# One decode step of gated attention plus MLP: fewer matmul instructions, two weight blocks moved in the load order

## The chip, the cores and the metric

The kernel runs on one core of a Trainium2 chip. The metric is device microseconds (us) of one execution. In what follows TensorE is called PE, VectorE DVE, ScalarE ACT, and SyncE SP; SP issues nearly all DMAs.

## The reference, cut to what matters

Two batch rows, one token each, D = 448, 16 heads of size 256, 4096 cached positions; all in float32.

```python
g = sigmoid((x * gate_w).sum(-1, keepdims=True))
q = (x @ wq).reshape(B, 1, 16, 256)
scores = einsum("bhqd,bhkd->bhqk", q, k_cache) * 256 ** -0.5
a = einsum("bhqk,bhkd->bhqd", softmax(scores), v_cache) @ wo
h = relu(x @ w1 + b1)
b = (h * h) @ w2 + b2
out = g * a + (1 - g) * b
```

The caches are 134 MB each, so nearly all of the 289.5 MB that the kernel reads is K and V, each byte of which is used once.

## The kernel before, in words

**Rounds.** The work is cut into 16 rounds, numbered 0 to 15 (`rounds`, `last` = 15). Round i is one batch row and one pair of heads; the two heads lie on the upper and the lower 64 partitions, 64 positions to a partition. Each round needs a K tile in two halves (`k{i}_0`, `k{i}_1`, 4 MB each, loaded by `load_k`, L141) and a V tile of 8 MB (`load_v`, L146; in round 15 `load_v_last` loads it as `va` and three pieces of `vb`, L152 and L156).

**What a round does.** DVE multiplies K by q in place (`times_q`, L303) and sums rows (`row_sums`, L308): two passes over each half. `maximum` (L312, L316) takes each partition's maximum and lets PE spread it over the partitions of its head; `softmax` reduces that to a negated maximum `nb` on DVE (L322) and exponentiates on ACT (L327). `values` (L353) multiplies the probabilities by V on PE with 32 matmuls, of which the trace shows two records each. `make_q` (L260, L263) spreads the q of the round after next over the partitions with PE and copies it with ACT. A few multiplications of the next round's K stand between the steps of the softmax, so that DVE needn't wait for PE.

**Units and output.** After a unit of four heads (after rounds 3, 7, 11) and after the last two pairs (rounds 13 and 15), `take` and `turn` (L367, L381, L390) bring the outputs on partitions; `project` (L394) multiplies four heads by their part of `wo`, accumulating in `acc` over 448 columns. For the last four heads (12 to 15) `late_wo`, and for the late blocks of `w2` `late_w2`, do the same product by `late` (L399), as four matmuls of 112 columns each into four row groups of `fin`. `w2` has 14 blocks of 224 KB; the first `WH` of them are multiplied into `acc` in round 4 (L472), the others at the very end. `ya` (L478) is the copy of `acc` that a `late` of its own adds to `fin`. Then `y4` (L500) leaves by two small DMAs.

**Memory and order of loads.** The order is written out by hand. SP issues the loads in program order, and each waits until its buffer is free. All of K, `w1`, `w2`, `wo` and `va` go through a ring of three buffers of 32 KB a partition; V, `wq` and `vb` share one buffer of 64 KB a partition. So V of round i is issued when PE is done with V of round i-1, and a half of K when DVE is done with the tile three ring places earlier. In round i SP issues V of round i, then extra weights if any, then `k{i+1}_1` and `k{i+2}_0`. The last K is issued in round 13; rounds 14 and 15 load V, the last part of `wo` (L125) and the late `w2` (L108).

Of the kernel before, what the change touches and what calls it, by code (L numbers as in the profile page):

```python
# [8 lines left out]
F32 = mybir.dt.float32  # L9
AF = mybir.ActivationFunctionType  # L10
ALU = mybir.AluOpType
# [5 lines left out]
def kernel(  # L17
# [32 lines left out]
    NQ = N // QB  # L50
    assert QB == 2 * DH
    DQ = D // 4
    WH = 2
    W2_CUTS = (4, 8, 11)
    V_CUTS = (48, 56)
    LEAD = 4
    LEAD2 = 16
# [11 lines left out]
    def slot(name):  # L69
        return ring.tile([P, J * DH], F32, name=name, tag="ring")  # L70
# [19 lines left out]
    w2_v = w2.rearrange("(p c) n -> p c n", c=FC)  # L90
    w2_sb = {}

    def w2_slot(lo, hi):
        t = slot(f"w2_{lo}")
        tv = t[:, :(hi - lo) * D].rearrange("p (c n) -> p c n", n=D)
        for c in range(lo, hi):
            w2_sb[c] = tv[:, c - lo, :]
        return tv

    def load_w2_early():  # L100
        tv = w2_slot(0, WH)
        nc.sync.dma_start(tv, w2_v[:, :WH, :])

    def load_w2_late():
        tv = w2_slot(WH, FC)
        at = [0, *W2_CUTS, FC - WH]
        for lo, hi in zip(at, at[1:]):
            nc.sync.dma_start(tv[:, lo:hi, :], w2_v[:, WH + lo:WH + hi, :])  # L108

# [4 lines left out]
    wo_sb = {}  # L116

    def load_wo(g):
        t = slot(f"wo{g}")
        tv = t[:, :HJ * D]  # L120
        if g < NG - 1:
            nc.sync.dma_start(tv, wo_g[g])
            wo_sb[g] = tv.rearrange("p (j n) -> p j n", j=HJ)
        else:
            nc.sync.dma_start(tv.rearrange("p (h k) -> p h k", h=HG), wo_v[:, g * HG:(g + 1) * HG, :])  # L125
            wo_sb[g] = tv.rearrange("p (h j n) -> p h j n", h=HG, j=NJ)


    rounds = [(b, n) for n in range(H // 2) for b in range(B)]
# [123 lines left out]
    def make_q(i):  # L253

        b, n = rounds[i]
        a, g = divmod(n, NQ // 2)
        r = 32 * g + B * a + b
        pq = ps.tile([P, 512], F32, name=f"pq{i}", tag="pq")
        for k in range(2):
            nc.tensor.matmul(pq[k * PH:(k + 1) * PH, :DH], ident[:, r:r + 1].to_broadcast([P, PH]),  # L260
                             qs[:, k * DH:(k + 1) * DH], start=True, stop=True)
        q_sb[i] = work.tile([P, DH], F32, name=f"q{i}", tag=f"q{b}")
        nc.scalar.activation(q_sb[i], pq[:, :DH], AF.Copy)  # L263


    hT = const.tile([P, FC, B], F32, name="hT")
# [43 lines left out]
    def maximum(i):  # L310
        m = work.tile([P, 1], F32, name=f"m{i}", tag="m")
        nc.vector.tensor_reduce(m, s_t[i], axis=AX.X, op=ALU.max)  # L312
        mt = ps.tile([P, 512], F32, name=f"mt{i}", tag="sm")
        for k in range(2):
            at = slice(k * PH, (k + 1) * PH)
            nc.tensor.matmul(mt[at, :PH], m.to_broadcast([P, PH]), ident[:, at], start=True, stop=True)  # L316
        return mt

    def softmax(i, mt):
        b, n = rounds[i]  # L320
        nb = work.tile([P, 1], F32, name=f"nb{i}", tag="nb")
        nc.vector.tensor_reduce(nb, mt[:, :PH], axis=AX.X, op=ALU.max, negate=True)  # L322
        u, k = unit_of[2 * n]
        for e in range(2):
            at = slice(e * PH, (e + 1) * PH)
            c = B * (k + e) + b
            nc.scalar.activation(pw[k, b][at, :, 2 * c:2 * c + 2], s_t[i][at].rearrange("p (m s) -> p m s", s=2), AF.Exp,  # L327
                                 bias=nb[at], accum_out=rs_t[u % 2][at, c:c + 1])
# [62 lines left out]

    def project(g):
        for j in range(HJ):
            nc.tensor.matmul(acc[:, :D], oT[g][:, j, :], wo_sb[g][:, j, :], start=False,  # L394
                             stop=(g == NG - 2 and j == HJ - 1))

    def late(lt, rhs, start=False, stop=False):
        for k in range(4):
            nc.tensor.matmul(fin[32 * k:32 * k + B, :DQ], lt, rhs[:, k * DQ:(k + 1) * DQ], start=start, stop=stop)  # L399

    def late_wo(h):
        u, k = unit_of[h]
        for j in range(NJ):
            late(oT[u][:, j, B * k:B * k + B], wo_sb[NG - 1][:, h % HG, j, :])

    def late_w2(lo, hi):
        for c in range(WH + lo, WH + hi):
            late(hT[:, c, :], w2_sb[c], stop=(c == FC - 1))
# [17 lines left out]
    for i, (b, n) in enumerate(rounds):  # L426
# [5 lines left out]
        if i == 1:  # L432
            w1_t = load_w1()
        if i == 4:
            load_w2_early()
        if done and u < NG - 1:
            load_wo(u)
        if i == last - 1:
            load_wo(NG - 1)
        if i == last:  # L440
            load_w2_late()
        if i < last - 1:
            load_k(i + 1, 1)
            load_k(i + 2, 0)
# [9 lines left out]
        if done:  # L454
            norm(u, sums(u))
        if i == last:
            break
        values(i, vt)

# [12 lines left out]
                nc.tensor.matmul(acc[:, :D], hT[:, c, :], w2_sb[c], start=False, stop=False)  # L472
        if i + 2 <= last:
            make_q(i + 2)
        if i == last - 3:

            ya = const.tile([B, D], F32, name="ya")
            nc.scalar.activation(ya, acc[:, :D], AF.Copy)  # L478
            late(ident[:B, :B], ya, start=True)
        if i == last - 1:  # L480
            late_wo(H - 4)
            late_wo(H - 3)
        rest(i + 1)
        if i == 2:
            ffn_square(pt)
# [6 lines left out]
    values(last, vt[1], p3, NK // 2)  # L492
    take(NG)
    turn(NG)
    late_w2(0, W2_CUTS[0])
    late_wo(H - 2)
    late_wo(H - 1)
    late_w2(W2_CUTS[0], FC - WH)
    y4 = const.tile([P, DQ], F32, name="y4")
    nc.scalar.activation(y4, fin[:, :DQ], AF.Copy)  # L500
    ov = out.rearrange("b s (k n) -> b k (s n)", k=4)
# [29 lines left out]
```

## Time and profile before

| | |
|---|---|
| median of 3 runs | 682.19 us (682.14 to 683.8) |
| the profiled execution, its own time | 683.37 us |
| its span, first to last instruction | 681.5 us |
| busy: DVE, PE, ACT | 571.7, 242.7, 35.4 us |
| read from memory | 289.56 MB |
| busy share of 16 DMA engines by the SP queue | 98.9% |

The span is measured between the first and the last instruction; 1.9 us of the profiled time lie around it. The clock column in the rows below is the clock granted to TensorE, as a share of 2.4 GHz: 0.50 is its 1.2 GHz level.

### The profile page before, as it was taken

The page shows a single profiled execution, that of the slowest core. Times are in us where ns is not written, and L with a number is a line of the kernel's source. Part 1 is how long each engine was busy: PE and PEld are TensorE (multiplying, and loading weights), DVE is VectorE, ACT ScalarE, POOL GpSimd, SP SyncE. Part 2 cuts the span into 40 slices and gives each one's busy share as a digit, 9 for nine tenths or more (in the row PEclk, how much of TensorE's full clock was granted, in tenths as well). Part 3 has the DMA queues.
Part 4 walks back from the last instruction along what each step waited for, and adds up shares of the span by engine and source line. Part 5 has one row for each costly group of instructions (what it writes and reads, how often), then busy time and mean ns, then how long its engine had stood idle before and what let it go on. Part 6 is the DMA issues. An engine that isn't in the chain of part 4 may idle for free.

```text
span 681.5 us, 3765 instructions
## 1 busy us (share of the span) xinstructions
PE 242.7 (36%) x1618; PEld 83.6 (12%) x1618; DVE 571.7 (84%) x171; ACT 35.4 (5%) x110; POOL 0.7 (0%) x6
## 2 busy tenths in 40 slices
PE   2500506308158150504028450321406523060066
PEld 1100101004014010101004110000103100010023
DVE  3199999597987979798895979989795997989970
ACT  0100000100001000000001000000001000000000
POOL 0000000000000000000000000000000000000000
PEclk9955856758566585756657775565858757585589
DMA  9999999999999999999999999999999999999996
GB/s 378 435 458 419 430 456 410 453 410 427 456 397 454 415 447 439 411 456 412 450 407 433 442 420 442 425 444 423 443 435 413 450 414 452 413 431 451 400 409 251
DMA packets 9500, 289.79 MB, mean 425 GB/s; under 512 B 1158, under 2 KB 1292, under 8 KB 2316
## 3 DMA queue, kind: packets, MB, share of 16 engines
q1 hardware_dynamic: 9320, 289.54, 98.9%
q8 instruction: 12, 0.20, 0.1%
q10 hardware_dynamic: 164, 0.02, 0.0%
q14 instruction: 4, 0.03, 0.0%
HBM read 289.56 MB, written 0.00 MB: 425 GB/s over the span
## 4 chain that ended last, share of the span: by engine, by line
DMA 62%; DVE 21%; PE 16%; issue 0%; ACT 0%; SPq 0%
DMA v<-in_A_v_cache_dram 51%; PE po_buf L353 15%; DVE k L303 10%; DVE s L308 10%; DMA k<-in_A_k_cache_dram 6%; DMA wq<-in_A_wq_dram 3%; DMA w<-in_B_w_dram 2%; PE po_buf L223 1%; PE fin L399 0%; PE pq L260 0%; ACT qs L249 0%; SPq L108 0%; DVE nb L322 0%; ACT q L263 0%; SPq L141 0%
## 5 line engine op out<-in xcount | busy, mean ns | idle before, releaser
L303 DVE TENSOR_TENSOR k<-k,q 128x4096 f32<-128x4096 f32 (+3 forms) x63 | 281.6, 4485 | 81.5 <-DMA k<-in_A_k_cache_dram 62.1
L308 DVE TENSOR_REDUCE s<-k 128x32 f32<-128x8192 f32 x32 | 277.9, 8686 | 1.1
L353 PE MATMUL po_buf<-v,pw 128*16 128x512 f32 (+1 forms) x960 | 137.7, 738 | 150.6 <-DMA v<-in_A_v_cache_dram 150.6
L316 PE MATMUL mt<-ident,m 128*64 128x64 f32 x64 | 7.6, 329 | 248.3 <-DVE m L312 248.3
L353 PEld LDWEIGHTS po_buf<-v,pw 128*16 128x16 f32 (+1 forms) x960 | 30.9, 111 | 246.0 <-issue 209.6
L316 PEld LDWEIGHTS mt<-ident,m 128*64 128x64 f32 x64 | 5.0, 201 | 255.2 <-issue 212.4
L327 ACT ACTIVATE pw<-s,nb 64x64 f32<-64x64 f32 x32 | 11.2, 349 | 287.7 <-DVE nb L322 287.4
L394 PE MATMUL acc<-wo,oT 128*2 128x448 f32 x48 | 24.3, 673 | 2.5 <-ACT oT L387 2.5
L381 PE MATMUL ot<-rl,shared 128*128 128x8 f32 x96 | 17.7, 322 | 5.2 <-ACT shared L363 5.2
L381 PEld LDWEIGHTS ot<-rl,shared 128*128 128x128 f32 x96 | 17.2, 278 | 8.3 <-ACT shared L363 8.3
L263 ACT ACTIVATE q<-pq 128x256 f32<-128x256 f32 x16 | 6.1, 383 | 198.7 <-PE pq L260 198.6
L260 PE MATMUL pq<-qs,ident 128*64 128x256 f32 x64 | 10.7, 418 | 0.7 <-ACT qs L249 0.7
L223 PE MATMUL po_buf<-wq,xT 128*4 128x512 f32 x56 | 8.7, 791 | 4.9 <-DMA wq<-in_A_wq_dram 4.9
L363 ACT ACTIVATE shared<-po_buf 128x1024 f32<-128x1024 f32 x6 | 5.8, 1021 | 55.2 <-PE po_buf L353 55.2
L284 PEld LDWEIGHTS pt<-ident,shared 4*128 4x128 f32 x28 | 6.9, 336 | 0.9 <-issue 0.9
L284 PE MATMUL pt<-ident,shared 4*128 4x4 f32 x28 | 7.0, 380 | 0.0
L394 PEld LDWEIGHTS acc<-wo,oT 128*2 128x2 f32 x48 | 4.5, 98 | 20.1 <-issue 17.4
L353 PE MATMUL po_buf<-va,pw 128*8 128x512 f32 x32 | 6.2, 947 | 0.0
L327 ACT ACTIVATION_READ_ACCUMULATOR pw<-s,nb 64x1 f32 x32 | 5.9, 185 | 0.0
L333 PE MATMUL sum<-rs,ones_pp 128*128 128x8 f32 (+1 forms) x10 | 3.0, 369 | 8.1 <-ACT pw L327 8.1
L223 PE MATMUL ph<-w,xT 128*4 128x448 f32 x28 | 5.4, 539 | 0.0
L260 PEld LDWEIGHTS pq<-qs,ident 128*64 128x64 f32 x64 | 3.3, 138 | 11.6 <-issue 9.7
(64 smaller groups left out, 60.5 us busy)
## 6 DMA issues: line engine op xcount, KB each, us to landing
k<-in_A_k_cache_dram SPq DMA_DIRECT2D x32, 4096.0 KB, 31.0
wq<-in_A_wq_dram SPq DMA_DIRECT2D x1, 7168.0 KB, 19.8
wo<-in_A_wo_dram SPq DMA_DIRECT2D x4, 1792.0 KB, 33.7
va<-in_A_v_cache_dram SPq DMA_DIRECT2D x1, 4096.0 KB
w<-in_B_w_dram SPq DMA_DIRECT2D x1, 3136.0 KB, 32.3
vb<-in_A_v_cache_dram SPq DMA_DIRECT2D x1, 2048.0 KB
vb<-in_A_v_cache_dram SPq DMA_DIRECT2D x2, 1024.0 KB, 13.1
w<-in_B_w_dram SPq DMA_DIRECT2D x2, 896.0 KB, 13.6
```

Source lines behind the costliest of these rows:

```text
L223: nc.tensor.matmul(out[32 * g:32 * g + 2 * B, :width], xT[:, half, c].rearrange("p s b -> p (s b)"), t[:, (a * n + g) * width:(a * n + g + ...
L260: nc.tensor.matmul(pq[k * PH:(k + 1) * PH, :DH], ident[:, r:r + 1].to_broadcast([P, PH]), qs[:, k * DH:(k + 1) * DH], start=True, stop=True)
L263: nc.scalar.activation(q_sb[i], pq[:, :DH], AF.Copy)
L284: nc.tensor.matmul(pt[:, c, :], hv[:, c, :], ident[:2 * B, :2 * B], start=True, stop=True)
L303: nc.vector.tensor_tensor(kt, kt, q_sb[i].unsqueeze(1).to_broadcast([P, hi - lo, DH]), op=ALU.mult)
L308: nc.vector.tensor_reduce(s_t[i][:, half * J:(half + 1) * J], kts[i, half], axis=AX.X, op=ALU.add)
L316: nc.tensor.matmul(mt[at, :PH], m.to_broadcast([P, PH]), ident[:, at], start=True, stop=True)
L327: nc.scalar.activation(pw[k, b][at, :, 2 * c:2 * c + 2], s_t[i][at].rearrange("p (m s) -> p m s", s=2), AF.Exp, bias=nb[at], accum_out=rs_ ...
L353: nc.tensor.matmul(po[r:r + 4 * n, :], pw[k, b][:, m, :4 * n], vt[:, 2 * m:2 * m + 2, :].rearrange("p j d -> p (j d)"), start=(k == 0 and ...
L363: nc.scalar.activation(o_w[:, s], po_bufs[u % 2][:, s * DH:(s + 1) * DH].rearrange("r (p j) -> r j p", j=HJ).unsqueeze(2).to_broadcast([P, ...
L381: nc.tensor.matmul(ptv[:, j, :], ov[:, s, j, :], rl_t[u][:, :, s], start=(s == 0), stop=(s == 1))
L394: nc.tensor.matmul(acc[:, :D], oT[g][:, j, :], wo_sb[g][:, j, :], start=False, stop=(g == NG - 2 and j == HJ - 1))
```

## The change

- `make_q`: one matmul of 128x512 instead of two of 64x256; then ACT copies each half of the partitions by itself (two copies instead of one).
- `maximum` and `softmax`: one matmul of 128x128 instead of two of 64x64; then DVE reduces each half of the partitions by itself (two reductions instead of one).
- `w2`: eight blocks instead of two are loaded and multiplied in round 4, six instead of twelve at the end, in pieces of three, two and one.
- `wo` of heads 12 and 13 is loaded alone in round 14 and multiplied into `acc` behind `values` of round 14 (`project_pair`); `ya` is copied after that, and the `late` that adds it to `fin` stands in round 15 between the sums and the last `values`.
- `wo` of heads 14 and 15 is loaded behind the last V, into the ring buffer that the late `w2` has too (`end`), and multiplied ahead of the late `w2`.

```diff
-    WH = 2
-    W2_CUTS = (4, 8, 11)
+    WH = 8
+    W2_CUTS = (3, 5)
...
+    def load_wo_pair(t, h):
+        tv = t[:, :2 * NJ * D].rearrange("p (h k) -> p h k", h=2)
+        nc.sync.dma_start(tv, wo_v[:, h:h + 2, :])
+        for k in range(2):
+            wo_h[h + k] = tv[:, k, :].rearrange("p (j n) -> p j n", j=NJ)
...
+        nc.tensor.matmul(pq, ident[:, r:r + 1].to_broadcast([P, P]), qs, start=True, stop=True)
+        q_sb[i] = work.tile([P, DH], F32, name=f"q{i}", tag=f"q{b}")
         for k in range(2):
-            nc.tensor.matmul(pq[k * PH:(k + 1) * PH, :DH], ident[:, r:r + 1].to_broadcast([P, PH]),
-                             qs[:, k * DH:(k + 1) * DH], start=True, stop=True)
-        q_sb[i] = work.tile([P, DH], F32, name=f"q{i}", tag=f"q{b}")
-        nc.scalar.activation(q_sb[i], pq[:, :DH], AF.Copy)
+            at = slice(k * PH, (k + 1) * PH)
+            nc.scalar.activation(q_sb[i][at], pq[at, k * DH:(k + 1) * DH], AF.Copy)
...
-        for k in range(2):
-            at = slice(k * PH, (k + 1) * PH)
-            nc.tensor.matmul(mt[at, :PH], m.to_broadcast([P, PH]), ident[:, at], start=True, stop=True)
+        nc.tensor.matmul(mt[:, :P], m.to_broadcast([P, P]), ident, start=True, stop=True)
...
-        nc.vector.tensor_reduce(nb, mt[:, :PH], axis=AX.X, op=ALU.max, negate=True)
+        for e in range(2):
+            at = slice(e * PH, (e + 1) * PH)
+            nc.vector.tensor_reduce(nb[at], mt[at, at], axis=AX.X, op=ALU.max, negate=True)
...
+    def project_pair(h):
+        u, k = unit_of[h]
+        for e in range(2):
+            for j in range(NJ):
+                nc.tensor.matmul(acc[:, :D], oT[u][:, j, B * (k + e):B * (k + e + 1)], wo_h[h + e][:, j, :], start=False,
+                                 stop=(e == 1 and j == NJ - 1))
...
         if i == 4:
-            load_w2_early()
+            load_w2(slot("w2a"), 0, WH)
...
         if i == last - 1:
-            load_wo(NG - 1)
+            load_wo_pair(slot("wo12"), H - 4)
         if i == last:
-            load_w2_late()
+            t = slot("end")
+            load_wo_pair(t, H - 2)
+            load_w2(t[:, 2 * NJ * D:], WH, FC, W2_CUTS)
...
         if i == last:
+            late(ident[:B, :B], ya, start=True)
             break
...
-        if i == last - 3:
-
+        if i == last - 1:
+
+            project_pair(H - 4)
             ya = const.tile([B, D], F32, name="ya")
             nc.scalar.activation(ya, acc[:, :D], AF.Copy)
-            late(ident[:B, :B], ya, start=True)
-        if i == last - 1:
-            late_wo(H - 4)
-            late_wo(H - 3)
...
-    late_w2(0, W2_CUTS[0])
     late_wo(H - 2)
     late_wo(H - 1)
-    late_w2(W2_CUTS[0], FC - WH)
+    late_w2(0, FC - WH)
```

**SP's queue in rounds 3 to 5.** First before, then changed; `v_514` is V of round 4, the `k` names behind it are the second half of round 5 and the first of round 6.

```order
L146 DMA v_514<-in_A_v_cache_dram 128x16384
L102 DMA w_0_516<-in_B_w_dram 128x896
L141 DMA k_1_518<-in_A_k_cache_dram 128x8192
L141 DMA k_0_520<-in_A_k_cache_dram 128x8192
L146 DMA v_577<-in_A_v_cache_dram 128x16384
```

```order
L140 DMA v_514<-in_A_v_cache_dram 128x16384
L99 DMA w2a<-in_B_w_dram 128x3584
L135 DMA k_1_518<-in_A_k_cache_dram 128x8192
L135 DMA k_0_520<-in_A_k_cache_dram 128x8192
L140 DMA v_583<-in_A_v_cache_dram 128x16384
```

The load of `w2` ahead of all later K has 3584 columns of float32 a partition instead of 896.

**SP's queue at the end.** First before, then changed; `k_1_1143` is the last K, `v_1214` is V of round 14.

```order
L141 DMA k_1_1143<-in_A_k_cache_dram 128x8192
L146 DMA v_1214<-in_A_v_cache_dram 128x16384
L125 DMA wo_1216<-in_A_wo_dram 128x4x896
L152 DMA va<-in_A_v_cache_dram 128x8192
L156 DMA vb<-in_A_v_cache_dram 128x4096
L156 DMA vb<-in_A_v_cache_dram 128x2048 x2
L108 DMA w_2_1288<-in_B_w_dram 128x1792 x2
L108 DMA w_2_1288<-in_B_w_dram 128x1344
L108 DMA w_2_1288<-in_B_w_dram 128x448
```

```order
L135 DMA k_1_1143<-in_A_k_cache_dram 128x8192
L140 DMA v_1214<-in_A_v_cache_dram 128x16384
L118 DMA wo_1216<-in_A_wo_dram 128x2x896
L146 DMA va<-in_A_v_cache_dram 128x8192
L150 DMA vb<-in_A_v_cache_dram 128x4096
L150 DMA vb<-in_A_v_cache_dram 128x2048 x2
L118 DMA end<-in_A_wo_dram 128x2x896
L99 DMA end<-in_B_w_dram 128x1344
L99 DMA end<-in_B_w_dram 128x896
L99 DMA end<-in_B_w_dram 128x448
```

Half of the last `wo` load stands behind `vb` now, and of `w2` there are three pieces of 2688 columns together instead of four of 5376.

**PE's queue from the maximum of round 14 on.** First before, then changed; `v_1214` is V of round 14, `mt_1295` and `mt_1285` are round 15's maxima.

```order
L316 MATMUL mt_1220<-ident,m_1218 64x64 x2
L353 MATMUL po_buf_92<-v_1214,pw_0_99 8x512 x32
L399 MATMUL fin<-wo_1216,oT_1202 2x112 x16
L316 MATMUL mt_1295<-ident,m_1293 64x64 x2
L333 MATMUL sum_1302<-rs_107,ones_pp 128x4
L353 MATMUL po_buf_92<-va,pw_1_101 8x512 x16
L353 MATMUL po_buf_92<-vb,pw_1_101 8x512 x16
L381 MATMUL ot_1343<-rl_1307,o_1341 128x4 x4
L399 MATMUL fin<-w_2_1288,hT 2x112 x16
L399 MATMUL fin<-wo_1216,oT_1348 2x112 x16
L399 MATMUL fin<-w_2_1288,hT 2x112 x32
```

```order
L308 MATMUL mt_1220<-ident,m_1218 128x128
L347 MATMUL po_buf_92<-v_1214,pw_0_99 8x512 x32
L394 MATMUL acc<-wo_1216,oT_1202 2x448 x4
L308 MATMUL mt_1285<-ident,m_1283 128x128
L327 MATMUL sum_1292<-rs_107,ones_pp 128x4
L399 MATMUL fin<-ya,ident 2x112 x4
L347 MATMUL po_buf_92<-va,pw_1_101 8x512 x16
L347 MATMUL po_buf_92<-vb,pw_1_101 8x512 x16
L375 MATMUL ot_1337<-rl_1297,o_1335 128x4 x4
L399 MATMUL fin<-end,oT_1342 2x112 x16
L399 MATMUL fin<-end,hT 2x112 x24
```

Behind the last `ot` stand 40 matmuls instead of 64, all of them `wo` first; the four on `ya` stand ahead of the last `values`.

## Rows read from the trace of the kernel before

**Rows 1.** The page: the span, and two DMA queues (packets, MB, share of 16 engines).
```profile
span 681.5 us, 3765 instructions
...
q1 hardware_dynamic: 9320, 289.54, 98.9%
q8 instruction: 12, 0.20, 0.1%
```

**Rows 2.** A stretch: length, busy of PE, PEld, DVE, ACT, POOL, clock, DMA share, GB/s.
```profile
300.00:500.00 200.00, 66.61 (x410) 21.53 (x410) 177.51 (x44) 8.93 (x31) 0.00 (x0) 0.63 1.00 433
```

**Rows 3.** Who waited for whom: us in total, times, longest.
```profile
DVE k L303 <- DMA k<-in_A_k_cache_dram: 62.1, 13, 8.0
```

**Rows 4.** The chain that ended last: start us, us, what (pieces of it).
```profile
119.34 35.79 DMA v<-in_A_v_cache_dram
...
193.97 9.96 PE po_buf L353 x64
...
246.02 30.90 DMA v<-in_A_v_cache_dram
...
514.47 8.44 PE po_buf L353 x64
...
567.47 39.53 DMA k<-in_A_k_cache_dram
...
625.82 0.13 DVE nb L322
...
660.47 16.64 DMA w<-in_B_w_dram
```

**Rows 5.** The instructions from 600 us on: start us, us, which [idle before <-releaser].
```profile
607.02 8.69 DVE L303 TENSOR_TENSOR k<-k,q 128x8192 f32<-128x8192 f32 x1 [3.32 <-DMA k<-in_A_k_cache_dram]
...
655.20 1.28 SPq L156 DMA_DIRECT2D vb<-in_A_v_cache_dram  x3
...
659.63 0.22 DVE L312 TENSOR_REDUCE m<-s 128x1 f32<-128x64 f32 x1
...
662.16 6.18 PE L353 MATMUL po_buf<-va,pw 128*8 128x512 f32 x32
...
668.17 3.61 PE L353 MATMUL po_buf<-vb,pw 128*8 128x512 f32 x32
...
673.54 0.95 PE L399 MATMUL fin<-w,hT 128*2 128x112 f32 x32
673.64 0.18 ACT L390 ACTIVATE oT<-ot 128x8 f32<-128x8 f32 x1 [1.20 <-PE ot L381]
...
675.07 0.95 PE L399 MATMUL fin<-w,hT 128*2 128x112 f32 x32
...
677.15 0.95 PE L399 MATMUL fin<-w,hT 128*2 128x112 f32 x32 [1.13 <-DMA w<-in_B_w_dram]
```

**Rows 6.** Groups by shape: xcount, busy us, mean ns, idle before.
```profile
L260 PE MATMUL pq<-qs,ident 128*64 128x256 f32 x64 | 10.7, 418 | 0.7 <-ACT qs L249 0.7
L263 ACT ACTIVATE q<-pq 128x256 f32<-128x256 f32 x16 | 6.1, 383 | 198.7 <-PE pq L260 198.6
L472 PE MATMUL acc<-w,hT 128*2 128x448 f32 x4 | 1.7, 539 | 0.0
L399 PE MATMUL fin<-ya,ident 2*2 2x112 f32 x8 | 0.4, 253 | 1.0 <-ACT ya L478 1.0
```

**Rows 7.** DMA issues: xcount, KB each, median us to landing.
```profile
w<-in_B_w_dram SPq DMA_DIRECT2D x1, 448.0 KB, 17.1
```

**Rows 8.** Stretches near the end, columns as in rows 2.
```profile
658.00:660.00 2.00, 0.00 (x1) 0.04 (x1) 1.81 (x2) 0.00 (x0) 0.00 (x0) 1.00 1.05 410
...
662.00:664.00 2.00, 2.00 (x14) 0.58 (x17) 0.51 (x3) 0.00 (x0) 0.00 (x0) 0.50 0.96 397
...
668.00:670.00 2.00, 2.00 (x24) 0.50 (x20) 0.00 (x0) 0.00 (x0) 0.00 (x0) 1.00 1.00 422
...
676.00:678.00 2.00, 0.87 (x35) 0.60 (x32) 0.00 (x0) 0.00 (x0) 0.00 (x0) 1.00 0.05 18
```

More of the change, by code (lines that the diff above doesn't have):

```diff
@@ L91, with load_w2 @@
     w2_sb = {}
-    def w2_slot(lo, hi):
-        t = slot(f"w2_{lo}")
+    def load_w2(t, lo, hi, cuts=()):
         tv = t[:, :(hi - lo) * D].rearrange("p (c n) -> p c n", n=D)
@@ L97, in w2_slot @@
             w2_sb[c] = tv[:, c - lo, :]
[L98 to L108, printed above, removed]
+        at = [0, *cuts, hi - lo]
+        for a, e in zip(at, at[1:]):
+            nc.sync.dma_start(tv[:, a:e, :], w2_v[:, lo + a:lo + e, :])
     HJ = HG * DH // P
@@ L118, in load_wo @@
     def load_wo(g):
[L119 to L126, printed above, removed]
+        tv = slot(f"wo{g}")[:, :HJ * D]
+        nc.sync.dma_start(tv, wo_g[g])
+        wo_sb[g] = tv.rearrange("p (j n) -> p j n", j=HJ)
+    wo_h = {}
+    def load_wo_pair(t, h):
[3 more added lines that the diff above has]
+            wo_h[h + k] = tv[:, k, :].rearrange("p (j n) -> p j n", j=NJ)
     rounds = [(b, n) for n in range(H // 2) for b in range(B)]
@@ L393, in project @@
         for j in range(HJ):
-            nc.tensor.matmul(acc[:, :D], oT[g][:, j, :], wo_sb[g][:, j, :], start=False,
-                             stop=(g == NG - 2 and j == HJ - 1))
+            nc.tensor.matmul(acc[:, :D], oT[g][:, j, :], wo_sb[g][:, j, :], start=False, stop=False)
+    def project_pair(h):
[4 more added lines that the diff above has]
+                                 stop=(e == 1 and j == NJ - 1))
     def late(lt, rhs, start=False, stop=False):
@@ L403, in late_wo @@
         for j in range(NJ):
-            late(oT[u][:, j, B * k:B * k + B], wo_sb[NG - 1][:, h % HG, j, :])
+            late(oT[u][:, j, B * k:B * k + B], wo_h[h][:, j, :])
     def late_w2(lo, hi):
```

## The prediction

> **What bounds the kernel now.** I read the page's DMA queues first. SP's queue keeps 16 engines busy for 98.9% of the span [rows 1], and a long stretch in the middle shows a share of 1.00 at 433 GB/s [rows 2]. So the loads run one behind the other, without a hole, and when a tile lands is set by how many bytes stand ahead of it. Next I read who waits. DVE waited 13 times for a K tile, 62.1 us in all [rows 3]: it is faster than the loads and falls in step with them in every round. The last such wait is the one to remember: the second half of round 14's K landed at 607.0 us, after DVE had been idle for 3.32 us [rows 5]. The chain shows the same load, issued at 567.47 and 39.53 us under way [rows 4].
>
> From 607.02 on there are two paths to the end, and the timeline of the tail shows both [rows 5]. **The loads' path:** behind that K tile the queue still brings two halves of K, all of V of round 14, the last `wo`, V of round 15 and twelve blocks of `w2`; the third piece of `w2` is what PE waited for until 677.15, with 1.13 us of idle time. **The computing path:** DVE works without a gap from 607.02 until the last maximum, which starts at 659.63; the softmax of round 15 lets PE start the last `values` at 662.16; they end at 668.17 + 3.61 = 671.78; `oT` is ready at 673.64 + 0.18 = 673.82; then the final products follow. The loads' path ends last, but the computing path is only 1.13 us short of it. That slack is what this change has to be held against.
>
> **The change part by part.**
>
> *Six blocks of `w2` move from the end of the queue to round 4.* Two blocks are 448 KB [rows 7], so six are 1344 KB, 1.376 MB; at 433 GB/s [rows 2] that is 3.18 us. They are removed behind the last V and added ahead of every K and V from round 5 on. The sum of bytes is the same, so the end of the loads' path stays where it is. But every later K lands 3.18 us later, the one at 607.02 with them, at about 610.2. DVE was waiting for it and works without a gap afterwards, so nothing takes this up: **+3.18 us on the computing path**. From below: DVE's idle time before that tile is 3.32 us only because the earlier K are just as late; if part of the shift were taken up, it would be at rounds in which DVE doesn't wait, and there are none late in the run, so I take the whole. From above: 1.376 MB at 397 GB/s, the slowest of the busy stretches shown [rows 8], is 3.47 us. The Trainium skill (DMA: Bandwidth & Descriptors, section Where 436 GB/s comes from) says that loads from HBM are held to about 358 GB/s for a core; the rows show 433, so the trace disagrees. By the page's figure the blocks would cost an estimated 3.84 us, and the sum below would be 0.7 us more.
>
> PE's six further products in round 4 are 12 records at 1.7 us for 4 records [rows 6], under 5.1 us, behind `values` of round 4. SP's load of the ring buffer that they free waits for them; behind it stand the next loads. The cover is the queue: V issued at 246.02 landed 30.90 us later [rows 4], of which its own 8.39 MB take 19.4 us at 433 GB/s, so 11.5 us of older loads were still queued. Price 0 to 0; without that cover it would be up to 5.1 us.
>
> *Order of the last loads.* Half of the last `wo` (two heads, 0.92 MB, 2.1 us) goes behind V of round 15. The issue of `vb` waits for `values` of round 14, as before (655.20, [rows 5]), and its wait moves with everything else by 3.2 us. With less `wo` ahead of it, engines that run early may run dry for up to 2.1 us before `vb` comes. That is off the path, if the computing path ends last; the floor of the loads' path is the last landing. The `wo` of heads 14 and 15 lies ahead of `w2`, whose third piece was 16.64 us under way [rows 4]; it is needed only at the final products: 0.
>
> *One matmul and two copies for q.* The same columns go through PE (64 records of 256 become 32 of 512), and ACT gets one more copy of about 0.38 us in each round [rows 6]. From round 2 on, q is ready two rounds ahead: 0. The first q delays DVE's first product by about 0.4 us. SP's issues wait for DVE in the first rounds, but V issued at 119.34 landed 35.79 us later [rows 4], 16.4 us more than its own bytes take: the queue is deep, so 0; with an empty queue it would be 0.4.
>
> *One matmul and two reductions for the maximum.* PE's part has the same columns. DVE gets a second reduction per round, whose step in the chain is 0.13 us [rows 4]. In rounds 0 to 13 the waits for K, or in the first rounds the deep queue, hide it. In rounds 14 and 15 nothing does: **+0.26 us** (0.13 if ACT's first exponential starts after the first reduction).
>
> *`ya` moves in front of the last `values`.* Eight records, 0.4 us busy in all [rows 6] at the high clock, stand between the sums and `values`. They are pipelined with what follows, so **+0.3 us** (0.2 to 0.5). The products of heads 12 and 13 follow `values` of round 14 in both kernels, while PE waits for DVE: 0.
>
> *The last `values`.* Before they took 671.78 - 662.16 = 9.62 us: the granted clock had fallen from 1.00 to 0.50 (the 1.2 GHz level) after PE had little to do, and the `va` half took 6.18 us, the `vb` half at 1.00 3.61 us [rows 5, 8]. In the eleven earlier rounds that the chain lists with 64 records they took 8.44 to 9.96 us [rows 4], 9.13 in the mean. PE again has some 4 us with almost nothing to do before them, so the clock should fall again; when it rises within them is open. I take 9.13: **-0.49 us** (-1.18 to +0.34).
>
> *The final products.* Before, 6.32 us passed from the end of `values` (671.78) to the end of the last product (677.15 + 0.95 = 678.10). In the changed kernel `oT` takes the same 2.04 us. Then come 40 matmuls, 80 records. Records went through at 32 in (675.07 - 673.54) / 2 = 0.765 us [rows 5], so 1.91 us, and about 0.2 to drain: 4.15 us. **-2.17 us.** No `w2` fills the pause before `oT` any more; that is in the 4.15.
>
> *The sum.* Computing path: 3.18 + 0.26 + 0.3 - 0.49 - 2.17 = **+1.08 us** against the end at 678.10. Loads' path: the last landing stays at about 677.1 to 677.7, and only the last block (8 records, 0.2 us) can stand behind it, so it ends at about 677.95, 0.15 us before the old end. The computing path is now the later one, by 1.2 us. The profiled execution (span 681.5, its own time 683.37) would become 684.45. Its time lies 1.18 us above the median of the runs, 682.19; the difference carries over, so I forecast **683.3 us**, 0.16% above 682.19.
>
> **The rivals.** About 0.3%, 2.05 us, is what a measurement of this kernel can tell from no change.
>
> *A. The loads stay the bound.* If PE stays at the high clock through the last `values`, they take 2 x 3.61 = 7.2 us instead of 9.13, and the computing path ends 1.9 us sooner, at 677.3, ahead of the last `w2`. Then the loads' path decides: 682.19 - 0.15 = 682.0. For it: the clock was still 1.00 from 658 to 660 with an idle PE [rows 8], and the products of heads 12 and 13 take PE a little further. Against it: the clock did fall in the same pause before the last `values` [rows 8], and over the long stretch its mean is 0.63 [rows 2], as it would be if every pause brought it down.
>
> *B. Slower by more than 0.3%: PE late and slow in the last round.* The place is `values` of round 15 and the products behind it. If the clock rises late, `values` take 9.96 us as in the slowest round [rows 4]: +0.83 us, or 684.1. From 0.97 us above the forecast on it counts as slower, so another 0.14 us decides. That comes if the 80 final records find the clock at 0.50 for even a tenth of their way; all of them at 0.50 would be +1.9, or 686.0. For it: the path has no slack left in front of the output, so each tenth counts. Against it: at the end before, the clock stayed at 1.00 even through the wait of 1.13 us.
>
> *C. Fewer instructions help the queue.* PE fetches its instructions over the same DMA engines: 12 packets, 0.20 MB, 0.1% of the 16 engines' span [rows 1], or 0.00 to 0.15% at most, some 10.9 us of one engine, 0.9 us each. The change takes out 16 + 16 matmuls in the rounds, 12 by `wo` and 18 by `w2`, 62 in all; each is two matmul and two weight-load records, so 248 instructions. If each packet delays the engine that finishes last, the tiles come sooner by up to 0.9 us, and the time is 682.4; together with A it is 681.1. The Trainium skill (Runtime: NRT & Kernel Launch, section Instruction fetch mechanics) says that a sequencer refills in blocks of 256 instructions by its own DMA queue and that this is mostly hidden; the 12 packets of the trace agree with the block size, and by the page the gain would be an estimated one packet. Against a gain beyond 0.3%: it needs more than two packets on one engine.
>
> **How the numbers follow.** The forecast (computing path ends last, within 0.3%) has 0.62. A has 0.14, at 682.0, and also counts as same. B has 0.18, at 684.3 to 686. C in a form that brings more than 0.3%, below 680.1, has 0.03, and what I haven't seen 0.03, of which I give 0.01 to faster, 0.01 to same and 0.01 to slower. So same is 0.62 + 0.14 + 0.01 = 0.77, slower 0.19, faster 0.04. The range runs from the loads' floor, 682.0 less 0.2 for C, 681.8, up to 684.9 in B: the sum with the upper ends of its terms (3.47 for the shift, 0.5 for `ya`, +0.34 for `values`) is 3.47 + 0.26 + 0.5 + 0.34 - 2.17 = 2.40, 684.6, and 0.3 for a little of the final products at the low clock. About 0.1 lies above it and 0.06 below.
>
> **What would show it.** In the profile of the changed kernel: the wait of DVE for round 14's second half of K ends about 3 us later (610 instead of 607); the last maximum is at about 663; the last `values` start near 666; PE no longer waits for `w2` in the final products, and the chain of waits leads from the output through `fin`, `values` and DVE back to K instead of to the load of `w2`; the DMA share falls to nothing before the final products start. q8 shows 11 or 12 packets. It would be wrong if DVE's work after the last K started less than 2 us later, if the last `values` took 7.2 us, or if the chain still ended in a `w2` load.

## The result: slower, by 0.46%

| | median | runs |
|---|---|---|
| before | 682.18 us | 681.88 to 683.8 (10) |
| changed | 685.66 us | 683.82 to 687.06 (10) |
| ratio | 1.0046 | 95% interval 1.0031 to 1.0062 |

The forecast was 683.3 us, no measurable change, in a range up to 684.9; the time is 2.4 us above the forecast and outside the range. The ten runs of the changed kernel lie in two groups, five from 683.82 to 684.7 and five from 686.63 to 687.06, with nothing between them. So the median, 685.66 us, lies in the gap and is no execution's time; the medians of the two groups are 684.36 and 686.92 us, and the ratio of the two overall medians would be 1.0051. The profiled execution, 687.06 us with a span of 685.3, is from the upper group. Two more profiles of the kernel stand below, after_b and after_c; after_c, 684.17 us, is from the lower group.

The instructions of the changed kernel's profile (687.06 us) that answer to [rows 5]; columns are start, duration, instruction, idle time before it:

```profile
610.51 8.69 DVE L297 TENSOR_TENSOR k<-k,q 128x8192 f32<-128x8192 f32 x1 [2.42 <-DMA k<-in_A_k_cache_dram]
...
629.22 0.47 DVE L316 TENSOR_REDUCE nb<-mt 64x1 f32<-64x64 f32 x2
629.72 7.69 DVE L297 TENSOR_TENSOR k<-k,q 128x3072 f32<-128x3072 f32 x2
...
663.49 0.22 DVE L306 TENSOR_REDUCE m<-s 128x1 f32<-128x64 f32 x1
...
666.14 0.55 PE L399 MATMUL fin<-ya,ident 2*2 2x112 f32 x8
...
666.62 6.00 PE L347 MATMUL po_buf<-va,pw 128*8 128x512 f32 x32
...
672.44 3.61 PE L347 MATMUL po_buf<-vb,pw 128*8 128x512 f32 x32
...
678.14 1.60 PE L399 MATMUL fin<-end,oT 128*2 128x112 f32 x32 [0.27 <-ACT oT L384]
...
679.50 2.40 PE L399 MATMUL fin<-end,hT 128*2 128x112 f32 x48
```

DVE's last wait for K ends 3.49 us later than in [rows 5], and everything that follows is late with it. At the end no product waits for `w2` any more: only `oT` is waited for. The loads were done before: the rows below show a DMA share of 0.07 in the stretch before the products, and of 0.00 and 0.03 while they run. They also show the clock (columns as in [rows 2]):

```profile
658.00:660.00 2.00, 2.00 (x16) 0.42 (x5) 2.00 (x1) 0.00 (x0) 0.00 (x0) 1.00 0.25 98
...
676.00:678.00 2.00, 1.15 (x12) 1.02 (x8) 0.00 (x0) 0.68 (x2) 0.00 (x0) 1.00 0.07 25
678.00:680.00 2.00, 1.85 (x44) 1.65 (x48) 0.00 (x0) 0.09 (x1) 0.00 (x0) 0.57 0.00 0
680.00:682.00 2.00, 1.90 (x44) 1.35 (x36) 0.00 (x0) 0.03 (x1) 0.00 (x0) 0.58 0.03 8
```

Right when the final products begin, the clock falls to its 1.2 GHz level. The first row is the hole in the loads that the prediction allowed for, ahead of `vb`: a DMA share of 0.25 from 658 to 660. PE doesn't wait for `vb`, so the hole is off the path. The chain of waits, which before ended in the load of `w2` [rows 4], now runs through K, DVE, `values` and the products without a load behind K:

```profile
571.38 39.10 DMA k<-in_A_k_cache_dram
...
610.51 8.70 DVE k L297
...
629.46 0.23 DVE nb L316
...
666.69 9.41 PE po_buf L347 x64
...
678.14 3.80 PE fin L399 x80
...
681.97 0.26 ACT y L499
```

### The profile page after: what moved, and what is told of

Same layout as the page of the kernel before. It is cut to its first block, busy times and chain, and to the rows that moved or that the text cites. A ratio compares the mean times of both kernels' runs of the same rounds, so it can differ in the third digit from the quotient of the medians.

```text
span 685.3 us, 3560 instructions
## 1 busy us (share of the span) xinstructions
PE 260.6 (38%) x1494; PEld 86.3 (13%) x1494; DVE 577.9 (84%) x187; ACT 41.6 (6%) x126; POOL 0.7 (0%) x6
## 4 chain that ended last, share of the span: by engine, by line
DMA 59%; DVE 21%; PE 18%; ACT 0%; issue 0%; SPq 0%; ACTq 0%
DMA v<-in_A_v_cache_dram 51%; PE po_buf L347 16%; DVE k L297 10%; DVE s L302 10%; DMA k<-in_A_k_cache_dram 6%; DMA wq<-in_A_wq_dram 3%; PE po_buf L217 1%; PE fin L399 1%; DVE nb L316 0%; PE pq L253 0%; PE ot L375 0%; ACT pw L321 0%; ACT q L257 0%; ACT o L361 0%; ACT qs L243 0%
## 5 line engine op out<-in xcount | busy, mean ns | idle before, releaser
L308 PE MATMUL mt<-ident,m 128*128 128x128 f32 x32 | 11.7, 467 | 240.9 <-DVE m L306 240.9
L308 PEld LDWEIGHTS mt<-ident,m 128*128 128x128 f32 x32 | 7.6, 296 | 254.5 <-issue 211.3
L257 ACT ACTIVATE q<-pq 64x256 f32<-64x256 f32 x32 | 12.1, 378 | 211.2 <-PE pq L253 210.9
L253 PE MATMUL pq<-qs,ident 128*128 128x512 f32 x32 | 18.7, 671 | 0.7 <-ACT qs L243 0.7
L375 PE MATMUL ot<-rl,shared 128*128 128x8 f32 x96 | 15.4, 297 | 5.2 <-ACT shared L357 5.2
L375 PEld LDWEIGHTS ot<-rl,shared 128*128 128x128 f32 x96 | 14.9, 245 | 8.3 <-ACT shared L357 8.3
L316 DVE TENSOR_REDUCE nb<-mt 64x1 f32<-64x64 f32 x32 | 7.1, 221 | 1.5 <-PE mt L308 0.6
L253 PEld LDWEIGHTS pq<-qs,ident 128*128 128x128 f32 x32 | 5.0, 195 | 11.9 <-issue 10.2
L475 PE MATMUL acc<-w2a,hT 128*2 128x448 f32 x16 | 6.2, 539 | 0.0
```

Of the source, the lines that this page charges most:

```text
L253: nc.tensor.matmul(pq, ident[:, r:r + 1].to_broadcast([P, P]), qs, start=True, stop=True)
L257: nc.scalar.activation(q_sb[i][at], pq[at, k * DH:(k + 1) * DH], AF.Copy)
L308: nc.tensor.matmul(mt[:, :P], m.to_broadcast([P, P]), ident, start=True, stop=True)
L316: nc.vector.tensor_reduce(nb[at], mt[at, at], axis=AX.X, op=ALU.max, negate=True)
L375: nc.tensor.matmul(ptv[:, j, :], ov[:, s, j, :], rl_t[u][:, :, s], start=(s == 0), stop=(s == 1))
```

## The experiments

All ratios are against runs of the kernel before on the same chip, taken together with those of the experiment; their medians were 682.1 to 682.5.

**x1_two_early.** The changed kernel with two early `w2` blocks again:

```diff
-    WH = 8
-    W2_CUTS = (3, 5)
+    WH = 2
+    W2_CUTS = (4, 8, 11)
```

> The changed kernel with only the number of early w2 blocks put back: two in round 4, twelve at the end (three of the w2 pieces as before, all behind wo of heads 14 and 15). Everything else stays changed. Theory S (the shift: 1.38 MB moved ahead of K make every later K 3.2 to 3.5 us late, and DVE and PE behind the last K have no slack): the last wait of DVE for K ends at 607 again, the computing path comes 3.5 us sooner and gets 48 records of final products back (1.15 us at the high clock, 2.3 at the low one), so 682.2 to 684.0. Rival I (the instructions: two reductions, two copies, ya ahead of the last values cost the time): no gain, 684.3 or more.

Measured: 684.52 us, ratio 1.0024 (1.0012 to 1.0036), two runs at 682.47 and 682.76, one far off at 697.92, which the ratio leaves out, and five from 684.44 to 685.25. K is back at its old place:

```profile
607.12 8.69 DVE L297 TENSOR_TENSOR k<-k,q 128x8192 f32<-128x8192 f32 x1 [2.42 <-DMA k<-in_A_k_cache_dram]
...
675.17 1.20 PE L399 MATMUL fin<-end,oT 128*2 128x112 f32 x32 [0.27 <-ACT oT L384]
676.12 3.95 PE L399 MATMUL fin<-end,hT 128*2 128x112 f32 x96
```

The shift of K follows the six blocks, as theory S says. But the time is above the 684.0 that it allowed, and inside what rival I gave (684.3 or more): by the time alone this run speaks for I. The profile (685.25 us) shows two causes. From K to the last `values` it is 56.11 us, as in the changed kernel, where both profiles of before have 55.14 (this is I's part, below in x5). And the 128 records at the end take 4.90 us (675.17 to 680.07), in a stretch where the clock is 0.50 for a while (676 to 678), instead of the 3.06 that they would take at the rate of [rows 5]. So the load order alone isn't the whole cost.

**x2_only_w2.** The kernel before with only the number of early blocks changed:

```diff
-    WH = 2
-    W2_CUTS = (4, 8, 11)
+    WH = 8
+    W2_CUTS = (3, 5)
```

> The kernel before with only the number of early w2 blocks changed, eight in round 4 and six at the end; instructions and the place of wo as before. Theory S: K 3.2 to 3.5 us late, 40 records less at the end (0.96 us), against a slack of 1.1 us: 678.1 becomes some 679.5, so 683.4 to 684.0 where before is 682.2. Rival I: no change, 682.0 to 682.4.

Measured: 683.53 us, ratio 1.0020 (1.0012 to 1.0029), inside what theory S gave; rival I is out for this part.

```profile
610.42 8.69 DVE L303 TENSOR_TENSOR k<-k,q 128x8192 f32<-128x8192 f32 x1 [3.02 <-DMA k<-in_A_k_cache_dram]
...
677.08 0.76 PE L399 MATMUL fin<-w,hT 128*2 128x112 f32 x24
...
677.66 0.95 PE L399 MATMUL fin<-wo,oT 128*2 128x112 f32 x32
...
678.42 0.76 PE L399 MATMUL fin<-w,hT 128*2 128x112 f32 x24
```

K is 3.4 us late by this edit alone, and the products run without a wait for `w2`: the computing path ends last. Of these 3.4 us, 1.4 reach the time; the slack and the 48 records fewer at the end (not 40, as the expectation has it) take up the rest. These products, with `w2` ahead of `wo`, ran at a clock of 1.00.

**x3_w2_behind_k.** The changed kernel, with the six blocks loaded where no K stands behind them:

```diff
         if i == 4:
-            load_w2(slot("w2a"), 0, WH)
+            load_w2(slot("w2a"), 0, 2)
...
         if i == last - 1:
-            load_wo_pair(slot("wo12"), H - 4)
+            t = slot("wo12")
+            load_wo_pair(t, H - 4)
+            load_w2(t[:, 2 * NJ * D:], 2, WH)
...
+            for c in range(2, WH):
+                nc.tensor.matmul(acc[:, :D], hT[:, c, :], w2_sb[c], start=False, stop=False)
             project_pair(H - 4)
```

> The changed kernel with the same products and the same instructions, but six of the eight early w2 blocks are loaded in round 14, behind the last K and behind wo of heads 12 and 13, and multiplied into acc together with those. Theory S: no K is late, so the time falls back to the loads' floor or to the landing of the last V, 682.0 to 683.0. Rival I: unchanged, 684.3 to 686.9.

Measured: 682.89 us, ratio 1.0007 (0.9998 to 1.0015): of the 3.5 us that the change cost, some 2.7 are gone, with the same matmul instructions on PE, only six of them later. That is what theory S gave. Again there are two groups, five runs of 681.82 to 682.33 and six of 682.89 to 683.61; the profile, 682.98 us, is from the upper one and shows the final products at the low clock:

```profile
606.84 8.69 DVE L297 TENSOR_TENSOR k<-k,q 128x8192 f32<-128x8192 f32 x1 [2.43 <-DMA k<-in_A_k_cache_dram]
...
659.83 0.22 DVE L306 TENSOR_REDUCE m<-s 128x1 f32<-128x64 f32 x1
...
662.49 0.49 PE L308 MATMUL mt<-ident,m 128*128 128x128 f32 x2
...
664.90 3.62 PE L347 MATMUL po_buf<-va,pw 128*8 128x512 f32 x32
```

```profile
674.00:676.00 2.00, 1.96 (x48) 1.80 (x52) 0.00 (x0) 0.00 (x0) 0.00 (x0) 0.56 0.27 103
```

The edit undoes more than the shift, though. PE is busy with the products into `acc` until 662.5, so the matmul for the last maximum starts 2.66 us after that maximum, where the changed kernel has 0.37 (663.49 to 663.86); from the last maximum to the last `values` it is 5.07 us instead of 3.13. On the other side the clock stays at 1.00 through the last `values`, which take 7.05 us instead of 9.43. Against the profile of 687.06 us the last product ends 4.10 us sooner: 3.67 by K, 2.38 by `values`, less 1.94 on the way to them. The two side effects nearly cancel, and K is what remains.

**x4_fill.** The changed kernel with two more matmuls, whose results are not used, while ACT copies outputs:

```diff
+    fill = ps.tile([P, 512], F32, name="fill", tag="pq")
     take(NG)
+    nc.tensor.matmul(fill, ident, qs, start=True, stop=True)
     turn(NG)
+    nc.tensor.matmul(fill[:, :DH], ident, qs[:, :DH], start=True, stop=True)
     late_wo(H - 2)
```

> The changed kernel with two matmuls more on PE whose results are not used, one of 128x512 while ACT copies the last outputs and one of 128x256 while ACT copies oT. The ten runs of the changed kernel lie in two groups, 683.8 to 684.7 and 686.6 to 687.1. Theory C (in the upper group the clock falls to 0.50 for the final products, which take 3.8 us instead of 1.9): with PE kept busy in front of them the upper group goes, all runs 683.8 to 685.0. Rival L (the groups come from the loads): both groups stay, median 684 to 687.

Measured: 684.87 us, ratio 1.0038 (1.0027 to 1.005), runs 684.33 to 685.5: the upper group is gone. Two of the five (685.1 and 685.5) are above the 685.0 that theory C allowed; the fill itself stands in the way for a few tenths. In its profile the products run at 1.00:

```profile
677.22 0.95 PE L399 MATMUL fin<-end,oT 128*2 128x112 f32 x32
677.98 1.33 PE L399 MATMUL fin<-end,hT 128*2 128x112 f32 x48
```

```profile
676.00:678.00 2.00, 2.00 (x44) 1.67 (x47) 0.00 (x0) 0.18 (x1) 0.00 (x0) 1.00 0.02 6
678.00:680.00 2.00, 1.31 (x56) 1.04 (x44) 0.00 (x0) 0.26 (x1) 0.00 (x0) 1.00 0.04 8
```

80 records in 2.09 us, where the changed kernel's first profile has 3.76 (678.14 to 681.90).

**x5_short_path.** The changed kernel with the maximum of before, and `ya` added to `fin` in round 14:

```diff
-        nc.tensor.matmul(mt[:, :P], m.to_broadcast([P, P]), ident, start=True, stop=True)
+        for k in range(2):
+            at = slice(k * PH, (k + 1) * PH)
+            nc.tensor.matmul(mt[at, :PH], m.to_broadcast([P, PH]), ident[:, at], start=True, stop=True)
...
-        for e in range(2):
-            at = slice(e * PH, (e + 1) * PH)
-            nc.vector.tensor_reduce(nb[at], mt[at, at], axis=AX.X, op=ALU.max, negate=True)
+        nc.vector.tensor_reduce(nb, mt[:, :PH], axis=AX.X, op=ALU.max, negate=True)
...
         if i == last:
-            late(ident[:B, :B], ya, start=True)
             break
...
             nc.scalar.activation(ya, acc[:, :D], AF.Copy)
+            late(ident[:B, :B], ya, start=True)
```

> The changed kernel with the two parts undone that its profile shows on the computing path of the last rounds: the maximum as before (two matmuls, one reduction), and ya added to fin in round 14 instead of between the sums and the last values. The load order stays changed. Theory P (behind the last K nothing is hidden: the second reduction costs 0.37 us in round 14, the larger maximum 0.12 in round 15, ya 0.48): 0.97 us less than the changed kernel in either of its two groups, 683.4 and 685.9. Rival H (they lie beside other work): 684.4 and 686.9 as in the changed kernel.

Measured: 684.91 us, ratio 1.0041 (1.0028 to 1.0054), runs 683.92, 684.47, 684.91, 685.76, 685.97. If the two highest belong to the upper group, they are lower by about 1 us, as theory P says; the lower ones aren't. With five runs the time is inconclusive. The profile (683.92 us) does price the two parts: from the wait for K (610.17) to the last `values` (665.46) it is 55.29 us, where the changed kernel has 56.11 and, in after_c, 55.91. So they were worth 0.6 to 0.8 us on the path, instead of the 0.97 expected. But these `values` then took 9.18 us instead of the 8.48 of after_c, and the gain is lost in them.

**x6_instr_only.** The kernel before with only the fewer matmuls, for the maximum (the opposite of the first two pieces above) and for q:

```diff
-        for k in range(2):
-            nc.tensor.matmul(pq[k * PH:(k + 1) * PH, :DH], ident[:, r:r + 1].to_broadcast([P, PH]),
-                             qs[:, k * DH:(k + 1) * DH], start=True, stop=True)
+        nc.tensor.matmul(pq, ident[:, r:r + 1].to_broadcast([P, P]), qs, start=True, stop=True)
         q_sb[i] = work.tile([P, DH], F32, name=f"q{i}", tag=f"q{b}")
-        nc.scalar.activation(q_sb[i], pq[:, :DH], AF.Copy)
+        for k in range(2):
+            at = slice(k * PH, (k + 1) * PH)
+            nc.scalar.activation(q_sb[i][at], pq[at, k * DH:(k + 1) * DH], AF.Copy)
```

> The kernel before with only the fewer matmuls: one for a maximum with two reductions, one for q with two copies; loads and the end as before. Theory S and P together: K lands as before, the computing path gets 0.49 us longer and stays inside the slack of 1.1 us before the last w2, so 682.0 to 682.4, no difference from before. Rival I (the second reduction costs its 0.37 us in each of 16 rounds, or the larger matmuls slow PE): 0.4 to 5.9 us more, 682.6 to 688. Rival Q (fewer packets of instructions free the loads): 681.2 to 681.9.

Measured: 682.34 us against 682.12, ratio 1.0002 (0.9993 to 1.001). Rival I is out: the second reduction costs nothing in the rounds in which DVE waits. Behind the last K it does cost its 0.37 us here too (from 607.98 to the last maximum at 660.96 it is 52.98 us, before 52.61); the slack ahead of `w2` takes it, and the last products run without a wait of PE for the load:

```profile
675.84 1.83 PE L399 MATMUL fin<-w,hT 128*2 128x112 f32 x64
```

Fewer instructions bring nothing that can be seen, so rival Q is out too: the page still lists 12 packets of instructions, for this kernel and for the changed one, as [rows 1].

**x7_w2_first.** The changed kernel with the order of before in the final products:

```diff
+    late_w2(0, W2_CUTS[0])
     late_wo(H - 2)
     late_wo(H - 1)
-    late_w2(0, FC - WH)
+    late_w2(W2_CUTS[0], FC - WH)
```

> The changed kernel with the first three late w2 blocks multiplied ahead of wo of heads 14 and 15, as the kernel before does, in the pause in which ACT copies oT. Theory C (the final products lose about 2 us in the runs in which the clock falls before them): a third of the products moves into the pause, 0.2 to 0.3 us less in all runs, and the fall gets rarer: median 683.8 to 685.0. Rival L (the groups come from elsewhere): median 685.4, groups as in the changed kernel.

Measured: 684.93 us, ratio 1.0038 (1.0026 to 1.0051), runs 684.27 to 685.27. The upper group is gone here as well; the 0.2 to 0.3 us less in every run, which theory C also gave, can't be seen in the times. In the profile (685.04 us) the products start at 677.87, before ACT's copy of `oT` at 677.98, instead of behind it, and end 3.86 us behind `values` instead of 4.19 as in after_c; but `values` took 9.59 us.

```profile
677.87 0.76 PE L399 MATMUL fin<-end,hT 128*2 128x112 f32 x24
```

Of ten runs of x4 and x7 none is above 685.5, where five of ten of the changed kernel are above 686.6. The changed kernel itself wasn't run beside them; of the kernels taken together with x4 on the same chip, x1 and x3 have products at the low clock in their profiles.

**x9_mended.** x3 with the maximum of before and the product order of x7 (pieces as above).

> The changed kernel with six w2 blocks loaded behind the last K (as in x3_w2_behind_k), the maximum as before, and the first three late w2 blocks ahead of wo. If the shift of K, the parts on the last rounds' path and the order of the final products are all that the change costs, the loads decide again: 681.8 to 682.4, the time of before. If something else of the change costs time: 682.6 to 684.

Measured: 683.44 us, ratio 1.0013 (1.0004 to 1.0022), runs from 681.96 to 684.01: a miss. In its profile (684.01 us) the products wait for the first `w2` piece, which comes behind `wo` of heads 14 and 15, and then run at the low clock:

```profile
675.07 1.24 PE L399 MATMUL fin<-end,hT 128*2 128x112 f32 x24 [0.74 <-DMA end<-in_B_w_dram]
676.06 1.74 PE L399 MATMUL fin<-end,oT 128*2 128x112 f32 x32
677.56 1.27 PE L399 MATMUL fin<-end,hT 128*2 128x112 f32 x24
```

`w2` first helps only where `w2` is there first. And as in x3 the products into `acc` hold up the last maximum: its matmul starts at 663.19, 3.29 us after the maximum (659.90).

**x10_behind_k_fill.** x3 with the two fill matmuls of x4.

> x3_w2_behind_k with the two matmuls of x4_fill, whose results are not used. The eleven runs of x3_w2_behind_k lie in two groups, 681.8 to 682.3 and 682.9 to 683.6, and its profile, from the upper one, shows the clock at 0.50 in the final products. Theory C: with PE busy in front of them the upper group goes, all runs 681.8 to 682.5. Rival L (the upper group comes from the loads): both groups stay, median 682.9.

Measured: 682.30 us, all eleven runs between 681.83 and 682.66, ratio 0.9992 (0.9983 to 1.0002). With the blocks behind the last K and the clock held up, the kernel is back at the time of before, not measurably faster.

```profile
607.44 8.69 DVE L297 TENSOR_TENSOR k<-k,q 128x8192 f32<-128x8192 f32 x1 [2.42 <-DMA k<-in_A_k_cache_dram]
```

```profile
674.00:676.00 2.00, 2.00 (x57) 1.67 (x60) 0.00 (x0) 0.18 (x1) 0.00 (x0) 1.00 0.33 128
```

**after_b and after_c.** The changed kernel itself, for two more profiles.

> The changed kernel again, for a second profile. Theory C: if this execution takes 683.8 to 684.7, its final products (80 records) take 1.9 to 2.2 us at a clock of 1.00; if 686.6 to 687.1, 3.8 us at 0.50. Rival L: the products take the same in both, and the difference lies in the landing of K.

> The changed kernel once more, as after_b, so that one of the profiles is likely to come from the lower group. Theory C: 1.9 to 2.2 us for the 80 records at 1.00 in an execution of 683.8 to 684.7, 3.8 us at 0.50 in one of 686.6 to 687.1.

Measured: 685.28 and 684.17 us. after_c is in the lower group, and its products run at 1.00:

```profile
610.43 8.69 DVE L297 TENSOR_TENSOR k<-k,q 128x8192 f32<-128x8192 f32 x1 [2.42 <-DMA k<-in_A_k_cache_dram]
...
663.42 0.22 DVE L306 TENSOR_REDUCE m<-s 128x1 f32<-128x64 f32 x1
...
666.34 5.05 PE L347 MATMUL po_buf<-va,pw 128*8 128x512 f32 x32
...
671.21 3.61 PE L347 MATMUL po_buf<-vb,pw 128*8 128x512 f32 x32
...
676.92 0.95 PE L399 MATMUL fin<-end,oT 128*2 128x112 f32 x32 [0.27 <-ACT oT L384]
677.68 1.33 PE L399 MATMUL fin<-end,hT 128*2 128x112 f32 x48
```

80 records in 2.09 us (676.92 to 679.01), and K lands within 0.1 us of the 687.06 us execution: rival L falls, and between these two executions the products at the two clocks are the largest difference. after_b lies between the groups: its products took the same 2.09 us, its K landed 0.3 us later (610.75), and its `values` of round 15 ended 1.1 us later than in after_c.

**before_b.** The kernel before, for a second profile.

> The kernel before again, for a second profile. The first profiled execution took 683.37 us, the median of its runs is 682.2. Theory M (in that execution the last w2 landed about 1.1 us later than it usually does, so in a usual one both paths end together and the computing path has no slack): an execution of 682.0 to 682.4 shows no wait of PE for w2 over 0.3 us in the final products, and they end near 676.9. Rival N (profiled executions are about 1.2 us slower everywhere, with the same slack): PE waits about 1.1 us for w2 again, and an execution of about 682.2 shows the last K and the last values about 1.2 us earlier than the first profile.

Measured: 681.96 us. Neither theory held as written. K lands at 606.89, as in the first profile, so N is out. But PE still waits for `w2`, 0.74 us. What differs is the end of both paths: `values` took 8.80 us (662.03 to 670.83) instead of 9.62, and the awaited `w2` piece was there at 675.86 instead of 677.15:

```profile
606.89 8.69 DVE L303 TENSOR_TENSOR k<-k,q 128x8192 f32<-128x8192 f32 x1 [3.05 <-DMA k<-in_A_k_cache_dram]
...
662.03 4.97 PE L353 MATMUL po_buf<-va,pw 128*8 128x512 f32 x32
...
669.79 1.04 PE L353 MATMUL po_buf<-vb,pw 128*8 128x512 f32 x8 [0.22 <-DMA vb<-in_A_v_cache_dram]
...
675.86 0.95 PE L399 MATMUL fin<-w,hT 128*2 128x112 f32 x32 [0.74 <-DMA w<-in_B_w_dram]
```

## Why the prediction was wrong, by its own steps

| from the profiles, us | before, 683.37 | before_b, 681.96 | changed, 687.06 | after_c, 684.17 |
|---|---|---|---|---|
| DVE's last wait for K ends | 607.02 | 606.89 | 610.51 | 610.43 |
| from there to the last maximum | 52.61 | 52.61 | 52.98 | 52.99 |
| to the start of the last `values` | 2.53 | 2.53 | 3.13 | 2.92 |
| `values` | 9.62 | 8.80 | 9.43 | 8.48 |
| to the end of the last product | 6.32 | 5.98 | 5.85 | 4.19 |
| end of the last product | 678.10 | 676.81 | 681.90 | 679.01 |

**What bounds it, and the shift of K: right.** Up to the last K the loads run without a hole, DVE falls in with them, and 1.38 MB ahead of K make it late. The forecast was 3.18 us; single pairs of profiles show 3.4 to 3.5 (x2 and the changed kernel against the first profile of before). A single pair can't tell this to a few tenths, since K's landing moved by 1.1 us between profiles with the same loads ahead of it (606.89 in before_b, 607.98 in x6). Taken together, the seven profiles with eight early blocks have K at 610.45 in the mean, the seven with two at 607.23: 3.2 us, as forecast. The computing path took over the end, as forecast. By itself the shift costs 1.4 us (x2); with it undone in the changed kernel (x3) most of the cost goes. All the signs that the prediction named for itself came true (K at 610.5, the last maximum at 663.5, `values` at 666.6, the chain back to K), and none of those against it: they test the path, not the sizes along it.

**The step that failed first: "the difference carries over".** The sum itself came out close: it gave an execution of 684.45 us, and after_c took 684.17. Then I took off 1.18 us, because the profiled execution of before lay that much above the median. But that 1.18 us was not something that every execution profiled carries. before_b, 681.96 us and so close to the median, has the same K (0.13 us apart) and the same DVE work; in the first profile `values` were long and the last `w2` late by 1.3 us, and since the loads decided there, the late `w2` set that time. The changed kernel's end doesn't hang on `w2`, so but for the 0.13 us of K nothing was to be taken off. Of the 2.4 us between the forecast and the median, 1.18 are this subtraction; the other 1.2 are there because half of the runs lie in the upper group. That the sum came so close is partly luck: against the first profile of before, the shift and the smaller terms came out 0.4 us larger in after_c than I had them, and `values` 0.65 us shorter. Measured against before_b, whose last product ends at 676.81, that of after_c, from the lower group, ends 2.20 us later: 3.54 of shift (610.43 - 606.89), 0.38 and 0.39 on the way to `values`, -0.32 in `values`, -1.79 at the end. That is already slower by 0.32%. The slack of 1.13 us that I read from one profile was that of an execution with a late `w2`; in before_b it is 0.74, with `values` 0.8 us shorter. All this rests on one more profile of before.

**The term that was mis-sized: the final products.** I took 4.15 us from the end of `values` at the high clock. It was 4.19 in after_c, and 5.85 in the first profile, where the clock was at 0.50 for the products. That execution is from the upper group, in which half of the ten runs lie. This is the mechanism of rival B, to which I gave 0.18, with the argument that in the profile of before the clock stayed at 1.00 there. It did, but there `w2` products ran between `ot` and `oT`; the change took them away, which I noted as a matter of the sum and not as a cause of a fall. x4 and x7, which put work back in that place in two ways, have no run in the upper group, and x10 does the same for x3. The products' 1.7 us are less than the 2.6 us between the groups' medians (684.36 and 686.92). Between the two profiles of 687.06 and 684.17 us, 2.89 us apart, it is 1.66 in the products, 0.95 in `values` (9.43 and 8.48), 0.21 ahead of them and 0.08 in K. Only one execution of the upper group was profiled, so how much of the gap `values` make in general is open. Long `values` and slow products don't always go together: in after_b `values` took 8.77 us (667.16 to 675.93), and in x5, whose end is that of the changed kernel, 9.18, both ahead of fast products.

**Smaller terms.** The second reduction cost 0.37 us in round 14 instead of 0.13: between the start of `nb` and the next product lie 0.50 us (629.22 to 629.72), before 0.13. In round 15 and with `ya` it was 0.60, for 0.13 + 0.3 forecast; in after_c 0.39. Of the 0.60, `ya` is 0.48 (666.14 to 666.62), and 0.13 lie between the last maximum and `nb` (663.49 to 664.36, 0.87 us instead of 0.74): there PE's one matmul of 128x128 takes 0.46 us instead of the 0.34 of the two, a term that the prediction put at nothing because the columns are the same. The second reduction itself costs nothing in round 15: the first exponential starts 0.30 us after `nb`, before 0.31. In x6 the 0.37 us stand in the trace as well, but the slack takes them; x5 prices them in its trace and not in its time. `values` were forecast at 9.13; 9.43 and 8.48 are inside the bounds given.

**The rivals.** A, with the loads as the bound, would have needed the clock to hold through the last `values`; it fell to 0.50 in all three profiles of the changed kernel. It did hold in x3, where six products on `w2` fill PE's pause, and there `values` took 7.05 us instead of 8.5 to 9.4. C found nothing: 248 records less, and still 12 packets.

**What isn't settled.** What decides in which execution the clock falls in front of the products: the same program shows both. The runs only show that none of 21 with work in the pause (x4, x7, x10) lies in an upper group, and that `w2` products put there don't help when PE waits for their load (x9).

## What to carry to other kernels

Where a queue is full from end to end, moving bytes forward in it is a delay of everything behind them, however little work the moved bytes cause; put them behind the last tile that a busy engine waits for, as x3 and x10 do, and mind that their products don't then hold up that engine's chain, as the last maximum in x3. When a change lets another path end last, add up that path in absolute terms and in more than one execution; a difference taken against the old bound carries along what was accidental in that bound. And work in a pause in front of a train of small matmuls isn't free to take out: without it, half of the runs lie 2.6 us higher, and in the one of them that was profiled the products took 1.7 us more.

## What the runs showed of the hardware

The same product takes PE more than three times as long with a quarter of the instructions. `wo` of heads 12 and 13 by `late`, four matmuls of 112 columns in four row groups of `fin`, took 0.94 us in the profile of before; as one matmul of 448 columns into `acc`, 3.17 us in the changed kernel (a row of each, both at a clock of 1.00):

```profile
654.95 0.94 PE L399 MATMUL fin<-wo,oT 128*2 128x112 f32 x32
```

```profile
658.74 3.17 PE L394 MATMUL acc<-wo,oT 128*2 128x448 f32 x8
```

The Trainium skill (TensorEngine Tiling (Array Packing), section Theoretical Speedup) gives up to four times where a small dimension of the product is at most 32; here the output has two rows, and these two rows of the trace agree, with 3.4. In the changed kernel it cost nothing, since PE was waiting for DVE; in x3, with six such products on `w2` ahead of it, it stood in front of the last maximum.
